# An attention and gated-layer kernel on one core: one decay transfer a pair, other places for conversions, x loads and second products

## The chip, the cores and the metric

The kernel runs on 1 core of one Trainium2 chip. The metric is the device time of one execution in microseconds (us). Times of the kernel before are the median of 3 runs, and one profiled execution stands beside them.

## The reference

```python
def _attn_ref(q, k, v, f):                     # q, k, v: (4, 8, 576, 64), f: (4, 8, 576)
    scores = (1 / np.sqrt(D)) * np.matmul(q, k.transpose(0, 1, 3, 2))
    cum = np.cumsum(np.log(np.clip(f, 0.0001, 1.0)), axis=-1)
    decay = cum[:, :, :, None] - cum[:, :, None, :]
    scores = np.where(causal, -1000000000.0, scores + decay)   # causal: np.triu(ones, k=1)
    attn = np.exp(scores - np.max(scores, axis=-1, keepdims=True))
    return np.matmul(attn / (np.sum(attn, axis=-1, keepdims=True) + 1e-09), v)

x = np.ascontiguousarray(attn_out.transpose(0, 2, 1, 3)).reshape(B * S, H * D)  # (2304, 512)
x = (1 / (1 + np.exp(-(x @ w_gate))) * (x @ w_val)) @ w_out                     # d_ff 1536
h = x @ w_in
return (h * np.clip(h + 3.0, 0.0, 6.0) / 6.0) @ w_out2                          # d_ff 2048
```

The weights come as float64 words, read as pairs of int32.

## The kernel before

Every product of the two layers is three matmuls (`mm3`, lines 453 to 455): high part times high part, high times low, low times high. So each weight tile and each activation exists as a high and a low half.

**Attention.** The 32 heads are 16 pairs. A pair has five query units: four of 128 rows (units 0 to 3) and a tail of 64 rows for each of the two heads (unit 4), which share one tile. The 80 units run in a software pipeline, one step t a unit: scores and exponentials of unit t, the division (`norm`, POOL, L382) of unit t-1, the transposes (`flip`) of unit t-2, the products with v (`values`) of unit t-3. Pairs 0 to 6 walk their units upwards, with the tail last; pairs 7 to 15 walk downwards, with the tail first. The decay needs the cumulated logarithms along the keys in every partition: `dc` [128, 2 x 512] for the four full units, filled by two broadcast DMAs a pair (L266), and `dt` [128, 576] for the tail, with one head in each half of the partitions, filled by two more (L274). `dt` has a single buffer, `dc` two. The first pass over the scores is the reduction at L350 on DVE, which adds `dc` or `dt` to the scores in PSUM and takes the minimum. In pairs 0 to 6 the causal mask is added by small bf16 matmuls (L336 for full units, L343 with `mask2` for the tail); in the others POOL writes it into `dc` and `dt` (`hide`, L316 and L311).

**Conversions.** A weight tile is converted by two jobs. A job is a DMA of the raw words (L100), three passes on DVE (L103, L104, L110), a scaling on ACT (L107), the high half on POOL or ACT (L61, L63) and the low half on POOL (L64). The raw tiles have three buffers. 16 jobs run beside attention (from step 17, 0.7 of a job a step), 20 more up to the first chunk of the gated layer, and 32 are for the second layer. In the gated layer `CB` gives the jobs a feature block: 2.0 in its first chunk and 0.5 in all others.

**Beside attention** the tensor engine also computes four of the twelve feature blocks of the gated layer for the token chunks 0 to 2 (the `Filler`), whose x comes back from DRAM after the stores of a batch (`fill.load`, L174).

**The two layers.** A chunk is 512 tokens, the last one 256. `layer` walks chunks and, in each, feature blocks of 128: the up products of block f (`ups`), then the down products of block f-1 (`last`). Between the two, ACT, DVE and POOL make the activation and split it into `gall`, a ring of three buffers. The gated layer goes through the chunks 3, 4, 0, 1, 2, the second layer through 3, 0, 1, 2, 4. `up2` and `downs` ask for their weight (`conv.need`), which issues what is left of the jobs up to it.

**What sets the order.** The text gives a program order; a scheduler that simulates the engines then places the instructions of each engine, and every engine executes its own in that order. All transfers named here are issued by SP, in one queue in order.

Of the kernel before, what the change touches and what calls it, by code (L numbers as in the profile page):

```python
# [7 lines left out]
F32 = mybir.dt.float32  # L8
F32R = mybir.dt.float32r
BF16 = mybir.dt.bfloat16  # L10
I32 = mybir.dt.int32
AF = mybir.ActivationFunctionType
ALU = mybir.AluOpType
# [3 lines left out]
BIG = 1.0e30  # L17
# [3 lines left out]
def attn_moe_kernel(  # L21
# [57 lines left out]
    )  # L79

    mask2 = const.tile([P, TAIL], BF16, name="mask2")
    nc.gpsimd.memset(mask2, 0.0)
    for g in range(2):
        nc.gpsimd.affine_select(
            out=mask2[64 * g : 64 * g + 64], in_=mask2[64 * g : 64 * g + 64],
            compare_op=ALU.is_ge, fill=BIG, base=0, pattern=[[-1, TAIL]], channel_multiplier=1,
        )

# [152 lines left out]
    class Pair:  # L241
# [13 lines left out]
        def load(self):  # L255

            new = lambda nm: nat.tile([P, NKT, 2, D], F32, tag="nat", name=nm)
            self.qn = load_nat(new("qn"), q, self.b, self.hp, ())
            self.kn = load_nat(new("kn"), k, self.b, self.hp, ((0, k), (TAIL, q)))
            self.vn = load_nat(vns[self.i % 3], v, self.b, self.hp, ((TAIL, v),))  # L260

        def load_decay(self):
            h0 = self.b * H + 2 * self.hp
            self.dc = a2.tile([P, 2, NQ * P], F32, tag="dc", name="dc")
            for j in range(2):
                nc.sync.dma_start(  # L266
                    self.dc[:, j, :], cum_d[h0 + j : h0 + j + 1, : NQ * P].to_broadcast([P, NQ * P])
                )

        def load_tail_decay(self):  # L270
            h0 = self.b * H + 2 * self.hp
            self.dt = a1.tile([P, S], F32, tag="dt", name="dt")
            for j in range(2):
                nc.sync.dma_start(  # L274
                    self.dt[64 * j : 64 * j + 64, :], cum_d[h0 + j : h0 + j + 1, :].to_broadcast([64, S])
                )
# [26 lines left out]
        def hide(self, s):  # L303


            if self.pemask:
                return
            if s == NQ:
                for j in range(2):
                    d = self.dt[64 * j : 64 * j + 64, NQ * P : S]  # L310
                    nc.gpsimd.affine_select(  # L311
                        out=d, in_=d, compare_op=ALU.is_ge, fill=BIG, base=0, pattern=[[-1, TAIL]], channel_multiplier=1
                    )
            else:
                d = self.dc[:, :, s * P : (s + 1) * P]
                nc.gpsimd.affine_select(  # L316
                    out=d, in_=d, compare_op=ALU.is_ge, fill=BIG, base=0, pattern=[[0, 2], [-1, P]], channel_multiplier=1
                )

        def scores(self, s):  # L320
# [18 lines left out]
            for c, st in enumerate(self.sts):  # L339
                masked = self.pemask and c == 1  # L340
                nc.tensor.matmul(st[:, :hs], self.qz, self.kp[:, c * hs : (c + 1) * hs], start=True, stop=not masked)
                if masked:
                    nc.tensor.matmul(st[:, hs - TAIL : hs], identb, mask2, start=False, stop=True)  # L343

# [249 lines left out]
    def layer(src, order, feats, ups, downs, finish, rate, first, more=None):  # L594
# [7 lines left out]
        load(order[0], KC)  # L602
        last = None
        for ci, c in enumerate(order):
# [5 lines left out]
            for f in fs:  # L610
                gt = gall[:, ring["g"] % 3, :, :T]
                ring["g"] += 1
                ups(f, loaded[c], gt, T)
                if nxt is not None and f == fs[-1]:
                    load(nxt, KC)
                if last:
                    last()

                def last(f=f, gt=gt, outs=outs, c=c, T=T, fs=fs):
                    downs(f, gt, outs, T, f == fs[0], f == fs[-1])  # L620
                    if f == fs[-1]:
                        finish(outs, c, *chunks[c])

                if more:
                    more(ci, f)
                conv.run(rate(ci), EF)
        last()

# [12 lines left out]
    def ff1(w, order, first):  # L641
# [34 lines left out]
        def more(ci, f):  # L676
            if ci == len(order) - NCA - 1 and f == 2 * NGA:
                next_weights(3 * NGA)
            if ci == len(order) - 1 and f % 2 == 1:
                next_weights(2 if f == 2 * NGA + 1 else 3)  # L680

        feats = lambda c: range(2 * NGA if c < NCA else 0, nf)
        layer(x_d, order, feats, ups, downs, finish, lambda ci: CB[min(ci, 1)], first, more)

# [44 lines left out]

    CA, C0, CF, CB, CC = 0.7, 17, 0.9, (2.0, 0.5), 1.5  # L730

# [23 lines left out]
    pairs[0].load_decay()  # L755
    pairs[0].load_tail_decay()
    warm_up(WU)
    pairs[0].prep()
    done = 0
    for t in range(len(units) + 3):  # L760
# [3 lines left out]
        if t < len(units):  # L764
# [3 lines left out]
            if i == 0 and nxt:  # L768
                nxt.load()
                nxt.load_decay()  # L770
            p.scores(s)
            p.expo(s)
            if s > 0:
                p.hide(s - 1)
            if nxt and i == (len(p.order) - 1 if p.up else 2):
                nxt.load_tail_decay()
            if nxt and i == len(p.order) - 1:
                nxt.hide(NQ)
        if 1 <= t <= len(units):
# [5 lines left out]
        if t >= 3:  # L785
# [3 lines left out]
            if s == p.order[-1]:  # L789
                p.store()  # L790

                fill.load(p.b, p.hp + 1)
                if p.hp == NP - 1 and p.b < NCA:
                    done = p.b + 1
        if t < len(units):
# [4 lines left out]
        if t >= C0:  # L800
            conv.run(CA, EA)
        fill.n = done
# [63 lines left out]
```

## Time and profile before

| | us |
|---|---|
| median of 3 runs (1100.93 to 1103.43) | 1102.96 |
| the profiled execution | 1099.57 |
| its span in the trace | 1097.8 |

The profiled execution is the one that the rows below come from. Its time is 1.8 us longer than the span, which runs from the first to the last event of the trace. The attention stage, with its filler, takes the first third of the span, the gated layer ends near 690 us, and the second layer follows to the end. A gap in square brackets at the end of a row is the idle time of that engine right before the instruction and what ended it. A matmul's duration includes its place in a pipeline: how many were done in a stretch says more than their mean length. In the rows of busy time, PEclk is the granted clock of the tensor engine as a share of full speed: 1.00 is 2.4 GHz and 0.50 is 1.2 GHz.

### The profile page before, as it was taken

The page shows a single profiled execution, that of the slowest core. Times are in us where ns is not written, and L with a number is a line of the kernel's source. Part 1 is how long each engine was busy: PE and PEld are TensorE (multiplying, and loading weights), DVE is VectorE, ACT ScalarE, POOL GpSimd, SP SyncE. Part 2 cuts the span into 40 slices and gives each one's busy share as a digit, 9 for nine tenths or more (in the row PEclk, how much of TensorE's full clock was granted, in tenths as well). Part 3 has the DMA queues.
Part 4 walks back from the last instruction along what each step waited for, and adds up shares of the span by engine and source line. Part 5 has one row for each costly group of instructions (what it writes and reads, how often), then busy time and mean ns, then how long its engine had stood idle before and what let it go on. Part 6 is the DMA issues. An engine that isn't in the chain of part 4 may idle for free.

```text
span 1097.8 us, 15036 instructions
## 1 busy us (share of the span) xinstructions
PE 1058.7 (96%) x5383; PEld 833.7 (76%) x5383; DVE 541.6 (49%) x1174; ACT 349.1 (32%) x790; POOL 251.4 (23%) x357
## 2 busy tenths in 40 slices
PE   8889989999999999999999999999999999999998
PEld 4556765766766778998888888876888888888897
DVE  5588676435434872625234251699433333333343
ACT  5666466457353430312112020244211111111121
POOL 3366565224323430212102020043000000000000
PEclk9899999999999999999999999999999999999999
DMA  7878666266234521405052250643300200110010
GB/s 185 256 197 257 207 208 181 85 168 173 73 130 137 152 79 38 175 18 194 1 169 100 77 173 16 225 139 121 106 10 1 84 31 1 58 39 1 20 39 19
DMA packets 111241, 119.09 MB, mean 108 GB/s; under 512 B 63232, under 2 KB 66304, under 8 KB 111168
## 3 DMA queue, kind: packets, MB, share of 16 engines
q1 hardware_dynamic: 111072, 118.00, 35.0%
q8 instruction: 42, 0.69, 0.3%
q14 instruction: 31, 0.25, 0.1%
q10 hardware_dynamic: 96, 0.15, 0.0%
HBM read 91.30 MB, written 26.81 MB: 108 GB/s over the span
## 4 chain that ended last, share of the span: by engine, by line
PE 76%; DVE 7%; DMA 6%; issue 4%; POOL 3%; ACT 2%; SPq 1%; ACTq 0%; POOLq 0%; DVEq 0%
PE po L454 9%; PE po L453 9%; PE po L455 9%; PE ph L453 5%; PE ph L454 5%; PE ph L455 5%; PE pv L453 4%; PE pv L454 4%; PE pv L455 4%; PE pv L439 4%; PE pg L453 4%; PE pg L454 4%; PE pg L455 4%; PE st L327 3%; PE tt L406 2%
## 5 line engine op out<-in xcount | busy, mean ns | idle before, releaser
L64 DVE TENSOR_TENSOR gall<-sg,gall 128x512 fp32r<-128x512 f32 (+1 forms) x140 | 96.0, 685 | 91.0 <-ACT gall L61 49.1
L61 ACT CAST gall<-sg 128x512 fp32r<-128x512 f32 (+1 forms) x80 | 46.2, 578 | 272.7 <-DVE sg L692 268.8
L691 DVE TENSOR_SCALAR sg<-ph 128x512 f32<-128x512 f32 (+1 forms) x80 | 50.9, 637 | 145.9 <-PE ph L455 145.7
L454 PE MATMUL ph<-x,wi 128*128 128x512 f32 (+1 forms) x320 | 117.9, 369 | 0.0
L455 PE MATMUL ph<-x,wi 128*128 128x512 f32 (+1 forms) x320 | 117.7, 368 | 0.0
L453 PE MATMUL ph<-x,wi 128*128 128x512 f32 (+1 forms) x320 | 117.0, 368 | 0.0
L453 PE MATMUL po<-w,gall 128*128 128x512 f32 x288 | 112.9, 393 | 2.0 <-ACT gall L61 1.9
L454 PE MATMUL po<-w,gall 128*128 128x512 f32 x288 | 113.0, 392 | 0.0
L382 POOL TENSOR_SCALAR e<-e,m 128x256 f32<-128x256 f32 (+4 forms) x144 | 84.4, 598 | 122.1 <-DVE m L380 60.3
L455 PE MATMUL po<-w,gall 128*128 128x512 f32 x288 | 102.8, 395 | 2.7 <-DVE gall L64 2.7
L358 ACT ACTIVATE e<-e,m 128x256 f32<-128x256 f32 (+4 forms) x144 | 83.9, 584 | 61.5 <-DVE m L350 55.5
L454 PE MATMUL po<-gall,wo 128*128 128x512 f32 (+1 forms) x240 | 89.9, 376 | 4.3 <-DVE gall L64 4.3
L650 DVE TENSOR_TENSOR sg<-sg,pv 128x512 f32<-128x512 f32 (+1 forms) x48 | 29.6, 617 | 128.2 <-PE pv L455 126.8
L453 PE MATMUL pg<-x,wg 128*128 128x512 f32 (+1 forms) x240 | 90.4, 379 | 2.1 <-ACT sg L648 2.1
L454 PE MATMUL pg<-x,wg 128*128 128x512 f32 (+1 forms) x240 | 89.8, 374 | 0.4 <-DMA x<-x_d 0.4
L455 PE MATMUL pg<-x,wg 128*128 128x512 f32 (+1 forms) x240 | 89.8, 374 | 0.0
L453 PE MATMUL pv<-x,wv 128*128 128x512 f32 (+1 forms) x240 | 89.3, 372 | 0.0
L454 PE MATMUL pv<-x,wv 128*128 128x512 f32 (+1 forms) x240 | 89.0, 371 | 0.0
L453 PE MATMUL po<-gall,wo 128*128 128x512 f32 (+1 forms) x240 | 87.9, 374 | 1.0 <-POOL gall L63 1.0
L455 PE MATMUL pv<-x,wv 128*128 128x512 f32 (+1 forms) x240 | 88.8, 370 | 0.0
L455 PE MATMUL po<-gall,wo 128*128 128x512 f32 (+1 forms) x240 | 88.5, 371 | 0.0
L63 POOL TENSOR_SCALAR gall<-sg 128x512 fp32r<-128x512 f32 (+1 forms) x60 | 39.1, 653 | 214.6 <-DVE sg L650 207.5
(110 smaller groups left out, 1921.3 us busy)
## 6 DMA issues: line engine op xcount, KB each, us to landing
x<-x_d SPq DMA_DIRECT2D x88, 256.0 KB, 3.7
raw<-in_moe_w_out_dram SPq DMA_DIRECT2D x28, 512.0 KB, 3.6
x_d<-x SPq DMA_DIRECT2D x32, 288.0 KB, 2.9
dc<-cum_d SPq DMA_DIRECT2D x32, 256.0 KB, 4.3
x_d<-xs SPq DMA_DIRECT2D x32, 256.0 KB, 3.3
raw<-in_moe_w_in_dram SPq DMA_DIRECT2D x16, 512.0 KB, 4.4
raw<-in_moe_w_gate_dram SPq DMA_DIRECT2D x12, 512.0 KB, 4.0
raw<-in_moe_w_val_dram SPq DMA_DIRECT2D x12, 512.0 KB, 4.5
```

Source lines behind the costliest of these rows:

```text
L61: nc.scalar.copy(hi, src)
L63: eng_hi.tensor_scalar(hi, src, 1.0, 1.0, ALU.mult, ALU.mult)
L64: eng_lo.tensor_tensor(lo, src, hi.bitcast(F32), ALU.subtract)
L327: mm = nc.tensor.matmul(st[:, :n], self.qp[r, qs], self.kp[r, :n], start=True, stop=not self.pemask)
L358: nc.scalar.activation(e, e, AF.Exp, bias=m[:, a : a + 1], scale=-1.0, accum_out=m[:, 2 + b : 3 + b])
L382: nc.gpsimd.tensor_scalar(e, e, m[:, 6 + j : 7 + j], 1.0, ALU.mult, ALU.mult)
L439: row(nc.tensor.matmul(o[64 * j : 64 * j + 64, q0:], self.vn[:, kt, j], e, start=(kt == 0), stop=(kt == nk - 1)), kt == 0 and j == 0)
L453: nc.tensor.matmul(o, wh, xh, start=first, stop=False)
L454: nc.tensor.matmul(o, wh, xl, start=False, stop=False)
L455: nc.tensor.matmul(o, wl, xh, start=False, stop=last)
L650: nc.vector.tensor_tensor(sg, sg, pv, ALU.mult)
L691: nc.vector.tensor_scalar(sg, ph, 3.0, 0.0, ALU.add, ALU.max)
```

## The change

One DMA a pair now brings both heads' 576 columns into `dc` (L260 of the changed kernel). `dt` is no longer transferred: `tail_decay` makes it from `dc` with two POOL selects of 64 x 576 a pair, in all pairs, which write the tail's mask at once, so `mask2`, its matmuls and the tail's `hide` go. The v loads stand behind the decay. The filler's x is fetched two steps later. Conversions in attention start at step 14, and the last four of the 16 come at 0.09 a step. In both layers the down products come two blocks behind the up products, with four buffers of `gall`. The gated layer's chunks convert 2.0 (first), 0.5 and, in the last, 2.5 jobs a feature block.

```diff
...
-    mask2 = const.tile([P, TAIL], BF16, name="mask2")
-    nc.gpsimd.memset(mask2, 0.0)
-    for g in range(2):
-        nc.gpsimd.affine_select(
-            out=mask2[64 * g : 64 * g + 64], in_=mask2[64 * g : 64 * g + 64],
-            compare_op=ALU.is_ge, fill=BIG, base=0, pattern=[[-1, TAIL]], channel_multiplier=1,
-        )
...
+        def load_v(self):
...
-            self.dc = a2.tile([P, 2, NQ * P], F32, tag="dc", name="dc")
-            for j in range(2):
-                nc.sync.dma_start(
-                    self.dc[:, j, :], cum_d[h0 + j : h0 + j + 1, : NQ * P].to_broadcast([P, NQ * P])
-                )
+            self.dc = a2.tile([P, 2, S], F32, tag="dc", name="dc")
+            both = cum_d[h0 : h0 + 2].rearrange("h s -> (h s)").rearrange("(o x) -> o x", o=1)
+            nc.sync.dma_start(self.dc.rearrange("p h s -> p (h s)"), both.to_broadcast([P, 2 * S]))
+        def tail_decay(self):
...
-        def load_tail_decay(self):
-            h0 = self.b * H + 2 * self.hp
...
-                nc.sync.dma_start(
-                    self.dt[64 * j : 64 * j + 64, :], cum_d[h0 + j : h0 + j + 1, :].to_broadcast([64, S])
+                r = slice(64 * j, 64 * j + 64)
+                nc.gpsimd.affine_select(
+                    out=self.dt[r], in_=self.dc[r, j], compare_op=ALU.is_ge, fill=BIG, base=NQ * P,
+                    pattern=[[-1, S]], channel_multiplier=1,
...
-            if self.pemask:
-                return
-            if s == NQ:
-                for j in range(2):
-                    d = self.dt[64 * j : 64 * j + 64, NQ * P : S]
-                    nc.gpsimd.affine_select(
-                        out=d, in_=d, compare_op=ALU.is_ge, fill=BIG, base=0, pattern=[[-1, TAIL]], channel_multiplier=1
-                    )
-            else:
+            if not self.pemask:
...
-                masked = self.pemask and c == 1
-                nc.tensor.matmul(st[:, :hs], self.qz, self.kp[:, c * hs : (c + 1) * hs], start=True, stop=not masked)
-                if masked:
-                    nc.tensor.matmul(st[:, hs - TAIL : hs], identb, mask2, start=False, stop=True)
+                nc.tensor.matmul(st[:, :hs], self.qz, self.kp[:, c * hs : (c + 1) * hs], start=True, stop=True)
...
-        last = None
+        late = []
...
-                gt = gall[:, ring["g"] % 3, :, :T]
+                gt = gall[:, ring["g"] % 4, :, :T]
...
-                if last:
-                    last()
+                if len(late) > 1:
+                    late.pop(0)()
...
+                late.append(last)
...
-        last()
+        for last in late:
+            last()
...
-            if ci == len(order) - NCA - 1 and f == 2 * NGA:
+            if ci == len(order) - NCA - 1 and f == 2 * NGA + 1:
...
-        layer(x_d, order, feats, ups, downs, finish, lambda ci: CB[min(ci, 1)], first, more)
+        layer(x_d, order, feats, ups, downs, finish, lambda ci: CB[0] if ci == 0 else CB[1] if ci < len(order) - 1 else CB[2], first, more)
...
-    CA, C0, CF, CB, CC = 0.7, 17, 0.9, (2.0, 0.5), 1.5
+    CA, C0, CF, CB, CC = 0.7, 14, 0.9, (2.0, 0.5, 2.5), 1.5
+    CS = 0.09
...
-    pairs[0].load_tail_decay()
+    pairs[0].load_v()
+    pairs[0].tail_decay()
...
+                nxt.load_v()
...
-                nxt.load_tail_decay()
-            if nxt and i == len(p.order) - 1:
-                nxt.hide(NQ)
+                nxt.tail_decay()
...
-                fill.load(p.b, p.hp + 1)
...
+        if t >= 5:
+            p, s = units[t - 5]
+            if s == p.order[-1] and t < len(units) + 3:
+                fill.load(p.b, p.hp + 1)
...
-            conv.run(CA, EA)
+            conv.run(CA if len(conv.jobs) > 2 * NSA - 6 * NGA else CS, EA)
```

Three places show how the order moves. In the rows, names and lines are each kernel's own, and "x2" is two alike in a row.

**SP, among the loads of the third to fifth pairs.** `qn`, `kn` and `vn` are loads for attention, `x_d` a store of attention's result, `x` the filler's load. Before:

```order
L266 DMA dc<-cum_d 128x512 x2
L231 DMA qn<-in_q_dram 128x4x64
L274 DMA dt<-cum_d 64x576 x2
L174 DMA x<-x_d_93 128x512
L231 DMA qn<-in_q_dram 128x4x64
L174 DMA x<-x_d_94 128x512
L266 DMA dc<-cum_d 128x512 x2
```

Changed:

```order
L260 DMA dc<-cum_d 128x1152
L223 DMA qn<-in_q_dram 128x4x64 x2
L92 DMA raw<-in_moe_w_gate_dram 128x2x512 x2
L92 DMA raw<-in_moe_w_val_dram 128x2x512
L260 DMA dc<-cum_d 128x1152
L223 DMA vn_133<-in_v_dram 128x4x64 x2
L432 DMA x_d_85<-x 128x576
```

The two `dt` transfers are gone from between the loads, `dc` is one DMA, and the filler's x no longer stands here.

**POOL, in the pairs that walk downwards.** `e<-e,m` is the division of a unit, by its width (576 is the tail); `dc<-dc` and `dt` are the masks. Before:

```order
L382 TENSOR_SCALAR e<-e,m 128x256 x2
L382 TENSOR_SCALAR e<-e,m 128x128 x2
L382 TENSOR_SCALAR e<-e,m 128x576
L316 AFFINE_SELECT dc<-dc 128x2x128
L382 TENSOR_SCALAR e<-e,m 128x512 x2
L316 AFFINE_SELECT dc<-dc 128x2x128
L311 AFFINE_SELECT dt<-dt 64x64 x2
L316 AFFINE_SELECT dc<-dc 128x2x128
```

Changed:

```order
L366 TENSOR_SCALAR e<-e,m 128x256 x2
L366 TENSOR_SCALAR e<-e,m 128x128 x2
L366 TENSOR_SCALAR e<-e,m 128x576
L268 AFFINE_SELECT dt<-dc 64x576 x2
L303 AFFINE_SELECT dc<-dc 128x2x128 x2
L366 TENSOR_SCALAR e<-e,m 128x512 x2
L303 AFFINE_SELECT dc<-dc 128x2x128
```

Two selects of 64 x 576 now stand behind the tail's division and in front of the next unit's, where two of 64 x 64 stood one unit later.

**DVE, the gated layer's last chunk.** `sg<-sg,pv` and `gall<-sg,gall` are a feature block's activation and its low half, `raw<-raw` the passes of conversions. Before:

```order
L650 TENSOR_TENSOR sg<-sg,pv 128x512
L64 TENSOR_TENSOR gall<-sg,gall 128x512
L650 TENSOR_TENSOR sg<-sg,pv 128x512
L64 TENSOR_TENSOR gall<-sg,gall 128x512
L650 TENSOR_TENSOR sg<-sg,pv 128x512
L64 TENSOR_TENSOR gall<-sg,gall 128x512
```

Changed:

```order
L636 TENSOR_TENSOR sg<-sg,pv 128x512
L102 SCALAR_TENSOR_TENSOR raw<-raw 128x512
L64 TENSOR_TENSOR gall<-sg,gall 128x512
L95 TENSOR_SCALAR raw<-raw 128x512
L96 SCALAR_TENSOR_TENSOR raw<-raw 128x512
L95 TENSOR_SCALAR raw<-raw 128x512
L102 SCALAR_TENSOR_TENSOR raw<-raw 128x512
L96 SCALAR_TENSOR_TENSOR raw<-raw 128x512
L95 TENSOR_SCALAR raw<-raw 128x512
L96 SCALAR_TENSOR_TENSOR raw<-raw 128x512
L102 SCALAR_TENSOR_TENSOR raw<-raw 128x512
L636 TENSOR_TENSOR sg<-sg,pv 128x512
```

Before, five feature blocks at the end of this chunk have no conversion between them; now seven to eight passes stand between the activations of two blocks. The jobs left for the second layer's first chunk go from 17 to 4, and 16 stand in this chunk.

## Rows read from the trace of the kernel before

**Rows 1.** Page, parts 1 and 4: busy time by engine; shares of the last chain.

```profile
PE 1058.7 (96%) x5383; PEld 833.7 (76%) x5383; DVE 541.6 (49%) x1174; ACT 349.1 (32%) x790; POOL 251.4 (23%) x357
...
PE 76%; DVE 7%; DMA 6%; issue 4%; POOL 3%; ACT 2%; SPq 1%; ACTq 0%; POOLq 0%; DVEq 0%
```

**Rows 2.** Stretches: from:to, length, busy of PE PEld DVE ACT POOL, PEclk, DMA, GB/s.

```profile
47.50:54.30 6.80, 6.62 (x32) 4.70 (x32) 3.40 (x16) 3.95 (x11) 3.67 (x7) 0.50 0.83 238
50.00:100.00 50.00, 43.75 (x283) 28.33 (x279) 39.65 (x121) 34.76 (x97) 29.30 (x39) 0.96 0.82 234
...
372.00:404.00 32.00, 27.74 (x118) 21.42 (x116) 28.59 (x35) 13.81 (x23) 15.45 (x13) 1.00 0.42 130
455.00:472.00 17.00, 16.01 (x131) 15.60 (x130) 13.22 (x19) 6.54 (x12) 7.67 (x8) 1.00 0.17 59
640.00:695.00 55.00, 55.00 (x244) 45.60 (x243) 17.26 (x25) 8.71 (x14) 8.69 (x10) 1.00 0.27 87
720.00:770.00 50.00, 45.40 (x185) 34.96 (x184) 45.64 (x64) 22.57 (x35) 20.52 (x14) 0.97 0.41 127
850.00:900.00 50.00, 50.00 (x222) 41.46 (x221) 18.63 (x27) 7.77 (x13) 0.00 (x0) 1.00 0.19 63
```

**Rows 3.** Timeline from 41 to 48 us: start, length, engine, line, idle before.

```profile
41.57 1.11 SPq L274 DMA_DIRECT2D dt<-cum_d  x2
...
46.13 0.46 DVE L350 CUSTOM_DVE_ANT_0 e<-st,dt 128x288 f32<-128x288 f32 x1 [4.17 <-DMA dt<-cum_d]
...
47.67 1.09 PE L400 MATMUL tt<-ident,e 128*128 128x128 f32 x4 [2.61 <-DVE qp L288]
```

**Rows 4.** Timeline from 131 to 146 us, where the walking order turns.

```profile
131.48 8.09 SPq L274 DMA_DIRECT2D dt<-cum_d  x4
...
137.23 0.46 DVE L350 CUSTOM_DVE_ANT_0 e<-st,dt 128x288 f32<-128x288 f32 x1 [1.98 <-DMA dt<-cum_d]
...
141.82 0.66 PE L413 MATMUL tt<-ident,e 128*128 128x128 f32 x4 [0.80 <-POOL e L382]
...
144.99 0.33 PE L415 MATMUL t<-ident,e 128*128 128x128 f32 x1 [1.10 <-ACT etB L419]
```

**Rows 5.** Waits: who waited for whom: us in total, times, longest.

```profile
DVE e L350 <- DMA dt<-cum_d: 6.1, 2, 4.2
...
PE po L454 <- DVE gall L64: 4.3, 6, 1.7
...
PE po L455 <- DVE gall L64: 2.7, 2, 1.6
```

**Rows 6.** Timeline around 702 and 768 us: first and last of 17 jobs.

```profile
702.70 0.33 SPq L100 DMA_DIRECT2D raw<-in_moe_w_out_dram  x1
...
768.51 1.31 POOL L64 TENSOR_TENSOR w<-raw,w 128x512 fp32r<-128x512 f32 x1 [2.79 <-ACT w L61]
```

**Rows 7.** DVE's groups: shape, count; busy us, mean ns; idle before.

```profile
L104 DVE SCALAR_TENSOR_TENSOR raw<-raw 128x512 int32<-128x512 int32 x68 | 64.0, 942 | 1.4
L110 DVE SCALAR_TENSOR_TENSOR raw<-raw 128x512 int32<-128x512 int32 x68 | 57.6, 848 | 16.3 <-ACT raw L107 16.2
L103 DVE TENSOR_SCALAR raw<-raw 128x512 int32<-128x512 int32 x68 | 43.4, 639 | 29.4 <-DMA raw<-in_moe_w_in_dram 14.0 <-DMA raw<-in_moe_w_gate_dram 10.0 <-DMA raw<-in_moe_w_out_dram 3.9
```

**Rows 8.** POOL's groups, in the same form.

```profile
L316 POOL TENSOR_SCALAR_AFFINE_SELECT dc<-dc 128x256 f32<-128x256 f32 x36 | 15.6, 434 | 46.2 <-DVE m L350 28.5 <-DMA dc<-cum_d 12.6 <-issue 2.1
L382 POOL TENSOR_SCALAR e<-e,m 128x576 f32<-128x576 f32 x16 | 13.7, 854 | 16.3 <-DVE m L380 7.9 <-ACT etA L419 5.1 <-ACT e L358 1.9
...
L311 POOL TENSOR_SCALAR_AFFINE_SELECT dt<-dt 64x64 f32<-64x64 f32 x18 | 5.1, 284 | 3.1 <-DMA dt<-cum_d 2.8
```

**Rows 9.** The mask matmuls of the tail, in the same form.

```profile
L343 PE MATMUL st<-mask,identb 128*128 128x64 bf16 x7 | 1.4, 193 | 0.0
```

**Rows 10.** L104 on DVE: duration in ns, least, median and greatest.

```profile
L104 DVE SCALAR_TENSOR_TENSOR raw<-raw x68: 678/694/1819, 64.1 to 765.1; 128x512 int32<-128x512 int32 x68
```

**Rows 11.** DMA issues: count, KB each, median us from issue to landing.

```profile
dc<-cum_d SPq DMA_DIRECT2D x32, 256.0 KB, 4.3
```

## The prediction, made before the changed kernel was run

> **What bounds the kernel now.** First the page. TensorE is busy 96% of the span, and the chain that ended last runs over it for 76%; DVE, DMA, issue and POOL share most of the rest [rows 1]. Busy time of pipelined matmuls hides small gaps, so I read stretches next, and count matmuls in them. From 850 to 900 us, where only 128 x 512 matmuls run and nothing is late, 222 start in 50 us: 0.2252 us each [rows 2]. From 640 to 695 us there are 244 in 55 us, the same pitch, so the last chunk of the gated layer has no gap, although 0.5 of a job a block is converted there [rows 2]. Against this pitch the other stretches show what is lost. From 720 to 770 us there are 185 matmuls, worth 41.7 us: 8.3 of 50 us are lost, while DVE is busy for 45.6 of them [rows 2]. From 372 to 404 us there are 118, worth 26.6 of 32: 5.4 lost; from 455 to 472 us 131, among them 256-wide ones, with PE busy for 16.0 of 17: 1.0 lost [rows 2]. Attention has shorter and mixed instructions, so there I read the timeline: DVE waits 4.2 us for the transfer of `dt` that SP issued at 41.57, and PE then has a gap of 2.6 us ahead of 47.67 [rows 3]. Right behind it, from 47.5 to 54.3, the granted clock is 0.50, the level of 1.2 GHz [rows 2]. The second such wait, 2.0 us at 137 us, stands where pair 6 (tail last) meets pair 7 (tail first) and both want the one `dt` [rows 4]. The two make up 6.1 us in the list of waits [rows 5]. Everything not named here I take to stay.
>
> **The change, part by part**, against the profiled execution's own 1099.57 us.
>
> *The tail's transfer goes.* At the first place the gap of 2.6 us goes with the wait [rows 3]. The slow stretch behind it: 32 matmuls in 6.6 us of PE at half the clock; from 50 to 100 us, at 0.96, 283 take 43.75, or 0.155 each, which makes 4.9 for 32 [rows 2]. So 1.7 us return if the clock does not fall; bounded by nothing (another gap brings the fall back) and 3.4 (half of 6.8). Term: -4.3, between 0 and -6.0. At the second place the select of pair 7 must still wait until the tail of pair 6 has read `dt`, but then takes two POOL instructions and no transfer. What PE waits for around it is 0.8 and 1.1 us [rows 4]. Term: -1.9, between 0 and -1.9. The other pairs show no such wait [rows 5], so there a faster `dt` frees nothing. One DMA of `dc` in place of two, with 1152 columns in place of 1024: its 4.3 us [rows 11] lie a whole pair ahead of use. I take nothing. If its landing comes late, it costs what `dt` cost (the first rival but one).
>
> *POOL makes the tail's decay.* Per pair two selects of 64 x 576. No row has the shape: from 64 columns (284 ns) to 256 (434 ns) the slope is 0.78 ns a column, which puts 576 at 0.68 us; the division of 128 x 576 takes 0.85 [rows 8]. 32 of them are 22 to 27 us, less the 18 that go (5.1 us): POOL gets 17 to 22 us more, where it is busy for 29.3 of 50 us at the densest [rows 2]. What stands behind them in POOL's order is the next unit's division, for which the transposes wait. If each pair's two, 1.4 to 1.7 us, lay on the path in all 16 pairs, that were 22 to 27 us. In the rows PE meets POOL's division only now and then, at 0.8 us in the row shown [rows 4], because the pipeline gives a unit's division a whole step until the transposes. Term: +2 (one or two pairs in which they stand in the way), between 0 and +27; the row nearest is the 0.8, hence the low value.
>
> *The tail's mask.* Seven matmuls of 0.19 us go, 1.4 us at most [rows 9]. They lie in the dense score stretch, but the reduction behind them was what PE waited for; term 0, between 0 and -1.4.
>
> *Down products two blocks later.* The lost 5.4 and 1.0 us of the stretches from 372 and 455 [rows 2] are of one kind: a block's down products come right behind the next block's up products and wait for the last half of `gall` from DVE (4.3 and 2.7 us over the whole trace [rows 5]), while DVE is busy for 28.6 of 32 us with conversions in between [rows 2]. With another whole block of up products between, 24 matmuls or 5.4 us, the same chain has time. The list names 7.0 us of such waits; what the two stretches lose is 6.4. I take -5.0, between 0 and -6.4: something of the first stretch is waiting for weights, which this edit doesn't hasten. The price is one more buffer of `gall`, and one more block of down products at the very end, of the same number of matmuls.
>
> *Conversions to the last gated chunk.* By the order, the second layer's first chunk has 17 jobs left before and 4 now. Before, they ran from 702.70 to 769.8, 67.1 us, or 3.95 us a job [rows 6]. The second layer eats four jobs in two blocks, 48 matmuls or 10.8 us at the pitch: 2.7 a job. So it is held back by the converting, and the 8.3 us are the outcome. With 4 left, nothing holds it. The jobs' new place: a block of the last chunk has 36 matmuls, 8.1 us, in which 2.5 jobs come. A job on DVE is 0.94 + 0.85 + 0.64 = 2.43 us [rows 7], so 6.1 a block, and DVE's other work there is 17.3 of 55 us, 2.5 a block [rows 2]; that 17.3 has a few of the old jobs in it, so 8.1 of 8.1 is too much by their share. It is tight, but two blocks of slack lie behind each activation now, and what does not fit only slides on into the second layer. Term: -6.5 of the 8.3, between 0 and -8.3. It counts on the activation not falling behind the conversions in DVE's order.
>
> *The rest.* The filler's x two steps later: it leaves SP's queue free around the store, and its user comes a batch later; 0. Earlier and thinner conversions in attention: the same 16 jobs, 0. The scheduler puts much else elsewhere, which no row prices; I allow 3 us either way.
>
> Sum: -4.3 - 1.9 + 2 - 5.0 - 6.5 = -15.7, which makes 1083.9 for a profiled execution. The median of before lies 3.4 above its profiled one (1102.96 against 1099.57), so about **1087** as a median.
>
> On the same resources, the trace shows that a pass of the conversions, L104, takes 0.69 us as a rule and up to 1.82 [rows 10]: at times it stands still for as long as another instruction takes. The Trainium skill ("SBUF — State Buffer", section "Who interferes with whom") says that a DVE instruction with two SBUF inputs and a GpSimd one that reads SBUF shut each other out, the second to issue waiting for the whole of the first. The trace agrees: L104 has two such inputs, and the 1.1 us above the usual 0.69 are the length of a POOL instruction. By the row alone the passes keep their mean, and the sum stands; by the rule each of the 32 selects can hold a DVE instruction for its own 0.68 to 0.85 us, 22 to 27 us of DVE in all, which would carry the time to that of the slower rival below if PE waited for DVE each time.
>
> **The rivals.**
>
> *The stall only moves* (conversions too dense). For: at the 3.95 us a job of the old place [rows 6], 2.5 jobs are 9.9 us a block of 8.1, which over the eight blocks of the chunk is 14 us too much; raw tiles have three buffers as before. Against: there POOL, ACT and DVE also served a layer with shorter blocks, and what slides has slack. What does not fit slides into the second layer at the old pace, the 6.5 shrink to nothing, and the sum is -9.2: 1090.4 profiled, about 1094.
>
> *The wait changes its name.* `dc` now carries the tail too, and a select waits for it on POOL, in front of the next divisions. For: the transfers are dense in the first 100 us (DMA share 0.82 [rows 2]), where `dt` was late. Against: it is issued a pair ahead. Then -4.3 and -1.9 are lost: 1090.1 profiled, about 1093.5.
>
> *POOL's selects come onto the path* (slower). The place is attention, the price 1.4 to 1.7 us a pair. It decides if the selects delay the division in all pairs and POOL's queue never catches up: +22 to +27 in place of +2, so +4 to +9 in sum, 1104 to 1109 profiled, about 1110 as a median. It outweighs the 17.7 us of gains from some 11 pairs on. For: selects stand right in front of divisions in the order, and DMA waits move to POOL. Against: POOL is idle for 20 of 50 us there [rows 2].
>
> *The edits do not do it*: the scheduler places the later down products and the conversions so that PE still meets the same waits. Then only the first term remains, 1095.3 profiled, about 1099.
>
> **How the numbers follow.** The forecast 0.53, its own range from 1080 to 1092. The stall moves 0.14, about 1094. The wait changes its name 0.12, about 1093. POOL on the path 0.13, about 1110. The edits do not do it 0.08, about 1099, a part of which lies within 0.2% (2.2 us, about what a measurement here can tell from no change). Faster by more than that: 0.53 + 0.14 + 0.12 and a part of the last, 0.81; same 0.06; slower 0.13. The range goes from 1076 (all upper bounds of the gains, 24.0 us, give 1079; the scheduler's 3 below it) to 1104, which leaves out most of the slower rival.
>
> **What would show it.** In the changed trace: no gap ahead of PE near 41 to 54 us and no granted clock of 0.50 there; no DVE wait at the first reduction of pair 7's tail for a transfer; 118 matmuls in some 27 us in the first gated chunk; in the last gated chunk 0.2252 us a matmul still, with DVE nearly full; and 222 matmuls in 50 us from the second layer's start on. Wrong it would be if POOL's selects head the list of what transposes wait for, if waits for `gall` show in the last gated chunk, or if the second layer begins with DVE busy for 45 of 50 us again.

## The result, and the profile after

| | before | changed |
|---|---|---|
| median of 4 runs, us | 1102.09 (1100.93 to 1103.43) | 1086.14 (1084.18 to 1086.25) |
| profiled execution's span, us | 1097.8 | 1082.4 |

The changed kernel is faster: the ratio is 0.9845, 95% interval 0.9827 to 0.9864. The forecast of 1087 us lies within a microsecond of it. Its parts don't: two gains were larger than predicted, and one, of 6.5 us, isn't there at all.

The page's parts 1 and 4 of the changed kernel (busy time by engine; shares of the last chain) answer to [rows 1]:

```profile
PE 1055.0 (97%) x5376; PEld 831.7 (77%) x5376; DVE 543.4 (50%) x1174; ACT 349.5 (32%) x790; POOL 273.7 (25%) x368
...
PE 82%; DVE 5%; DMA 5%; issue 3%; POOL 3%; ACT 2%; SPq 0%; ACTq 0%; POOLq 0%; DVEq 0%
```

POOL is busy for 22.3 us more: 17.5 are the new selects less those that went, and 5.0 are divisions that take longer (89.4 us in place of 84.4). PE's share of the chain rose. The stretches of the changed kernel (columns as in [rows 2]) say where:

```profile
41.00:54.00 13.00, 11.57 (x87) 7.04 (x83) 10.73 (x39) 9.24 (x28) 6.46 (x10) 1.00 0.89 231
50.00:75.00 25.00, 19.60 (x129) 11.16 (x127) 21.08 (x68) 18.48 (x55) 21.22 (x25) 0.93 0.81 235
131.00:146.00 15.00, 15.00 (x89) 10.00 (x89) 6.91 (x24) 8.63 (x22) 9.10 (x14) 1.00 0.27 83
360.00:392.00 32.00, 32.00 (x143) 26.48 (x142) 27.58 (x34) 13.07 (x22) 13.07 (x12) 1.00 0.48 153
440.00:460.00 20.00, 20.00 (x169) 20.00 (x169) 14.38 (x21) 7.04 (x13) 7.68 (x8) 1.00 0.35 121
622.00:650.00 28.00, 28.00 (x125) 23.17 (x125) 18.56 (x26) 8.73 (x14) 8.01 (x6) 1.00 0.66 213
650.00:665.00 15.00, 15.00 (x68) 12.43 (x67) 12.81 (x16) 5.70 (x9) 7.19 (x6) 1.00 0.46 149
665.00:690.00 25.00, 20.39 (x77) 15.62 (x76) 18.84 (x27) 10.67 (x17) 10.98 (x9) 0.86 0.66 220
712.00:762.00 50.00, 50.00 (x221) 41.08 (x220) 25.82 (x37) 9.42 (x15) 2.88 (x2) 1.00 0.01 4
```

At the pitch of 0.2252 us a matmul, the first gated chunk (360 to 392) and the turn of 440 to 460 lose nothing, and the second layer's start (712 to 762) loses 0.2 us, where before it lost 8.3 [rows 2]. But the end of the last gated chunk, gapless before, loses 7.7: 77 matmuls are worth 17.3 of its 25 us. The clock no longer falls at 41 to 54 us, and PE is busy throughout from 131 to 146. Attention's last product with v starts at 326.2 us, 7.6 earlier than the 333.8 of before. So the account of the two traces is: attention -7.6, the first gated chunk and the turn -6.4, the second layer's start -8.1, the last gated chunk +7.7. That makes -14.4 of the 15.4 us by which the spans differ.

The wait of the tail's reduction, [rows 5], in the changed kernel:

```profile
POOL dt L268 <- DMA dc<-cum_d: 21.8, 5, 9.9
...
ACT e L342 <- POOL dt L268: 1.5, 1, 1.5
...
DVE e L334 <- POOL dt L268: 0.6, 1, 0.6
```

The waiting for a transfer moved to POOL's selects, as a rival had it, but they are early enough: ACT and DVE wait for them once each, for 1.5 and 0.6 us. 9.9 of the 21.8 us are the first pair's, at the kernel's start.

How the 7.7 us are lost shows in the timeline of the changed kernel: DVE's activations (`sg`) and PE's waits between 640 and 690 us.

```profile
649.84 0.67 DVE L636 TENSOR_TENSOR sg<-sg,pv 128x512 f32<-128x512 f32 x1
659.60 0.68 DVE L636 TENSOR_TENSOR sg<-sg,pv 128x512 f32<-128x512 f32 x1
670.69 0.68 DVE L636 TENSOR_TENSOR sg<-sg,pv 128x512 f32<-128x512 f32 x1
673.34 0.49 PE L437 MATMUL po<-gall,wo 128*128 128x512 f32 x1 [1.95 <-POOL gall L63]
676.09 0.79 PE L438 MATMUL po<-gall,wo 128*128 128x512 f32 x1 [2.25 <-DVE gall L64]
679.94 0.68 DVE L636 TENSOR_TENSOR sg<-sg,pv 128x512 f32<-128x512 f32 x1
```

The products that these four activations read started their last matmul at 643.8, 652.0, 660.1 and 668.3 us. So the activation comes 6.0, 7.6, 10.6 and 11.6 us behind: it falls back from block to block until the slack of two blocks is used up, and PE waits for both halves of `gall`, at a clock that then falls as well.

### The profile page after: what moved, and what is told of

It is laid out like the page before. It is cut to its first block, busy times and chain, and to the rows that moved or that the text cites. A ratio compares the mean times of both kernels' runs of the same rounds, so it can differ in the third digit from the quotient of the medians.

```text
span 1082.4 us, 14927 instructions
## 1 busy us (share of the span) xinstructions
PE 1055.0 (97%) x5376; PEld 831.7 (77%) x5376; DVE 543.4 (50%) x1174; ACT 349.5 (32%) x790; POOL 273.7 (25%) x368
## 4 chain that ended last, share of the span: by engine, by line
PE 82%; DVE 5%; DMA 5%; issue 3%; POOL 3%; ACT 2%; SPq 0%; ACTq 0%; POOLq 0%; DVEq 0%
PE po L438 10%; PE po L439 9%; PE po L437 9%; PE ph L439 6%; PE ph L438 6%; PE ph L437 6%; PE pv L423 5%; PE st L314 4%; PE pv L438 3%; PE pv L437 3%; PE pv L439 3%; PE pg L439 3%; PE pg L438 3%; PE pg L437 3%; PE tt L390 2%
## 5 line engine op out<-in xcount | busy, mean ns | idle before, releaser
L438 PE MATMUL po<-w,gall 128*128 128x512 f32 x288 | 112.2, 390 | 0.0
L437 PE MATMUL po<-w,gall 128*128 128x512 f32 x288 | 112.1, 390 | 0.0
L439 PE MATMUL po<-w,gall 128*128 128x512 f32 x288 | 111.4, 389 | 0.0
L366 POOL TENSOR_SCALAR e<-e,m 128x256 f32<-128x256 f32 (+4 forms) x144 | 89.4, 634 | 75.1 <-DVE m L364 38.8
L438 PE MATMUL po<-gall,wo 128*128 128x512 f32 (+1 forms) x240 | 90.7, 379 | 2.7 <-DVE gall L64 2.7
L437 PE MATMUL po<-gall,wo 128*128 128x512 f32 (+1 forms) x240 | 89.7, 378 | 1.9 <-POOL gall L63 1.9
L439 PE MATMUL po<-gall,wo 128*128 128x512 f32 (+1 forms) x240 | 90.0, 377 | 0.0
```

The lines of the kernel that those rows point to most:

```text
L366: nc.gpsimd.tensor_scalar(e, e, m[:, 6 + j : 7 + j], 1.0, ALU.mult, ALU.mult)
L437: nc.tensor.matmul(o, wh, xh, start=first, stop=False)
L438: nc.tensor.matmul(o, wh, xl, start=False, stop=False)
L439: nc.tensor.matmul(o, wl, xh, start=False, stop=last)
```

## Experiments

Each time is a median, with the ratio to the runs of before in the same group. Losses of a stretch are its length less its matmuls times 0.2252 us.

**The decay part alone**, put into the kernel before (one DMA of `dc` a pair, two selects that make `dt`, no `mask2`; all else as before). A part of the edit:

```diff
...
-            self.dc = a2.tile([P, 2, NQ * P], F32, tag="dc", name="dc")
...
+            self.dc = a2.tile([P, 2, S], F32, tag="dc", name="dc")
...
-                nxt.load_tail_decay()
-            if nxt and i == len(p.order) - 1:
-                nxt.hide(NQ)
+                nxt.tail_decay()
...
```

> The kernel before with the decay part alone: one transfer a pair, the tail's decay by POOL selects, no mask2; v loads, x loads, conversions and down products as before. Theory A (the decay made the attention stage shorter): nearly all of the 7.7 us by which attention ended earlier in the changed kernel is here, about 1095 us, no DVE wait for a dt transfer, the last product with v near 326 us. Rival B (the moved x loads, v loads or conversions did it): 1099 or more, attention's end at 330 us or later.

1091.94 us, ratio 0.9894 (0.9877 to 0.991): 11.7 us. Attention's last product with v starts at 324.7. So theory A holds, and more than it asked for. Between the two profiled executions the difference is smaller, 7.2 us of span (1097.8 and 1090.6): attention ends 9.1 us earlier, and the layers take 2 us longer. The kernel before and this one, from 50 to 75 us:

```profile
50.00:75.00 25.00, 20.99 (x141) 12.76 (x138) 17.95 (x65) 17.99 (x53) 11.49 (x17) 0.91 0.82 225
```

```profile
50.00:75.00 25.00, 22.90 (x158) 14.27 (x158) 22.35 (x67) 18.82 (x56) 19.59 (x26) 1.00 0.76 225
```

There are 17 more matmuls, and the clock stays up throughout, while the prediction had priced its fall at the one place around 47 us only.

**The later down products alone**, put into the kernel before (with the fourth buffer of `gall` and the later `next_weights` that they need). A part of the edit:

```diff
...
-                if last:
-                    last()
+                if len(late) > 1:
+                    late.pop(0)()
...
```

> The kernel before with the down products two blocks later and four gall buffers alone. Theory: the stretches of the first gated chunk lose nothing any more (6.7 us come back) and 0.4 us at the end, about 1095 us; the second layer's start still loses 8 us. Rival (the first chunk waits for weights or conversions): half of it or less, 1099 or more.

1090.84 us, ratio 0.9884 (0.987 to 0.9899): 12.8 us, more than the theory. The first gated chunk and the second layer's start:

```profile
374.00:402.00 28.00, 28.00 (x125) 23.21 (x124) 23.04 (x29) 12.19 (x21) 11.89 (x10) 1.00 0.46 149
...
725.00:775.00 50.00, 48.02 (x201) 38.33 (x201) 38.54 (x56) 18.52 (x29) 14.13 (x10) 0.97 0.41 130
```

The first loses nothing. The second loses 4.7 us where before lost 8.3: the block of slack covers part of the conversion stall as well, which neither the theory nor the prediction had. These are 10.0 us; from the gated layer's first product to the end of the span, the two profiled executions differ by 11.3 (763.8 and 752.5).

**The denser conversions alone**, put into the kernel before:

```diff
-        layer(x_d, order, feats, ups, downs, finish, lambda ci: CB[min(ci, 1)], first, more)
+        layer(x_d, order, feats, ups, downs, finish, lambda ci: CB[0] if ci == 0 else CB[1] if ci < len(order) - 1 else CB[2], first, more)
...
-    CA, C0, CF, CB, CC = 0.7, 17, 0.9, (2.0, 0.5), 1.5
+    CA, C0, CF, CB, CC = 0.7, 17, 0.9, (2.0, 0.5, 2.5), 1.5
```

> The kernel before with 2.5 jobs a block in the last gated chunk alone; down products one block later as before. Theory (the stall only moves: 2.5 jobs a block hold the activation up in DVE's order): the 8.4 us at the second layer's start come back, and at least as much is lost in the last gated chunk, since only one block of slack is there: 1102 to 1112 us. Rival (the denser conversions are hidden, as predicted): about 1095 us.

1106.33 us, ratio 1.0025 (1.0007 to 1.0042): slightly slower. Its last gated chunk, the second layer's start, and PE's waits in the former:

```profile
675.00:715.00 40.00, 35.12 (x142) 26.98 (x141) 32.14 (x44) 16.21 (x26) 17.27 (x14) 0.96 0.54 177
720.00:770.00 50.00, 50.00 (x222) 41.17 (x221) 27.12 (x41) 10.76 (x17) 5.54 (x4) 1.00 0.18 59
```

```profile
PE po L454 <- DVE gall L64: 3.6, 3, 1.8
PE po L453 <- POOL gall L63: 1.2, 2, 0.7
```

8.0 of 40 us are lost in the one (142 matmuls are worth 32.0) and none in the other. The stall moved, with its size: 8.3 us at the second layer's start before, 8.0 in the last gated chunk now.

**The changed kernel with 0.5 jobs in the last gated chunk.**

```diff
-    CA, C0, CF, CB, CC = 0.7, 14, 0.9, (2.0, 0.5, 2.5), 1.5
+    CA, C0, CF, CB, CC = 0.7, 14, 0.9, (2.0, 0.5, 0.5), 1.5
```

> The changed kernel with 0.5 jobs a block in the last gated chunk, as before. Theory (the stall only moves): 8 us come back in the last gated chunk and about 8.4 are lost at the second layer's start, so the time stays within 2 us of the changed kernel's 1086. Rival (this edit is worth the predicted 6.5 us): about 1092.5 us.

1084.28 us (1081.78 to 1086.4), against 1086.14 and, in the next group, 1086.6 for the changed kernel: the edit is worth nothing, or costs a little. The last gated chunk and the second layer's start:

```profile
625.00:675.00 50.00, 50.00 (x222) 41.41 (x221) 18.87 (x28) 9.22 (x15) 8.99 (x9) 1.00 0.37 123
...
712.00:762.00 50.00, 47.43 (x199) 37.87 (x199) 43.02 (x62) 21.37 (x33) 17.23 (x12) 0.97 0.33 106
```

Nothing is lost in the first, 5.2 us in the second. In the changed kernel it is 7.7 and 0.2. So by these stretches the denser conversions cost 2.7 us, and by the medians 2.

**The small edits.** The changed kernel again as a reference, the two large parts together without the rest, and the changed kernel with one small edit undone each:

```diff
f2:
-    CA, C0, CF, CB, CC = 0.7, 14, 0.9, (2.0, 0.5, 2.5), 1.5
+    CA, C0, CF, CB, CC = 0.7, 17, 0.9, (2.0, 0.5, 2.5), 1.5
...
-            conv.run(CA if len(conv.jobs) > 2 * NSA - 6 * NGA else CS, EA)
+            conv.run(CA, EA)

f3:
...
+                fill.load(p.b, p.hp + 1)
...
-        if t >= 5:
-            p, s = units[t - 5]
-            if s == p.order[-1] and t < len(units) + 3:
-
-                fill.load(p.b, p.hp + 1)
...
```

In f3 the load stands right behind the store, two steps earlier.

> The changed kernel again, as a reference for the others of this group: 1084 to 1088 us.

> The kernel before with the decay part and the later down products together, without the other edits. If the two add (they took 11.7 and 12.8 us alone): about 1079 us, some 6 us below the changed kernel, and the edits left out cost what is missing. If they share their gain (rival): 1084 to 1086, and the edits left out cost nothing.

> The changed kernel with the conversions in attention as before (from step 17, 0.7 a step throughout). Theory (early conversions meet the tail's selects on POOL): PE's wait of 3.0 us at 66 us for a division that stands behind two conversion passes and two selects is gone, and the time is 2 to 4 us below the changed kernel's. Rival (the start is free): within 1 us of it.

> The changed kernel with the filler's x fetched right behind the store, as before. Predicted at nothing: within 2 us of the changed kernel. Rival (the later fetch keeps SP's queue free for the decay): 2 us or more above it.

| run | median, us | lowest to highest |
|---|---|---|
| the changed kernel again | 1086.60 | 1085.73 to 1088.27 |
| decay and downs alone (f1) | 1081.29 | 1079.18 to 1083.89 |
| old start of conversions (f2) | 1084.10 | 1082.53 to 1087.07 |
| x behind the store (f3) | 1089.75 | 1086.27 to 1093.28 |

The two parts almost add: 20.5 of 24.5 us (ratio 0.9805, 0.9762 to 0.9848). The other edits together cost 5.3 us. From the gated layer's first product to the end of the span, f1 takes 752.1 us and the changed kernel, in its two profiles, 756.0 and 755.3. So 3 to 4 us lie behind attention, most of them the cost of the denser conversions. The early start may take the rest: its medians differ by 2.5 us, as the theory had it, but the runs overlap, so this isn't shown. Its mechanism is seen. In the changed kernel, POOL and PE around 66 us:

```profile
63.76 1.09 POOL L63 TENSOR_SCALAR wv<-raw 128x512 fp32r<-128x512 f32 x1
64.93 1.30 POOL L64 TENSOR_TENSOR wv<-raw,wv 128x512 fp32r<-128x512 f32 x1
66.19 1.85 POOL L268 TENSOR_SCALAR_AFFINE_SELECT dt<-dc 64x576 f32<-64x576 f32 x2
68.13 1.92 POOL L366 TENSOR_SCALAR e<-e,m 128x576 f32<-128x576 f32 x3
68.98 0.66 PE L397 MATMUL tt<-ident,e 128*128 128x128 f32 x4 [3.01 <-POOL e L366]
```

The tail's division stands behind two conversion passes and two selects, and PE waits 3.0 us. The same wait of 3.0 us, with 129 matmuls from 50 to 75 us, stands in the second profile of the changed kernel. With the old start, the corresponding wait is 0.8 us, and 161 matmuls start:

```profile
50.00:75.00 25.00, 22.91 (x161) 14.08 (x158) 21.96 (x67) 19.17 (x56) 19.52 (x26) 1.00 0.78 226
```

The later x fetch seems to help by 3 us, against my nothing; the runs are too wide apart to be sure. The new place of the v loads was not tried by itself.

**Between 0.5 and 2.5 jobs a block**, with the old start of conversions in attention:

```diff
-    CA, C0, CF, CB, CC = 0.7, 14, 0.9, (2.0, 0.5, 2.5), 1.5
+    CA, C0, CF, CB, CC = 0.7, 17, 0.9, (2.0, 0.5, 1.0), 1.5
...
-            conv.run(CA if len(conv.jobs) > 2 * NSA - 6 * NGA else CS, EA)
+            conv.run(CA, EA)
```

The second run has 1.5 in place of 1.0.

> The changed kernel with the conversions in attention as before and 1.0 job a block in the last gated chunk in place of 2.5. Theory (at 2.5 the last gated chunk loses 8 us, at 0.5 the second layer's start loses 5; between them both fit): at most 3 us lost in both places together, 1079 to 1081 us. Rival (what is taken from one place is lost in the other at any rate): 1082 to 1085 us.

> As the run before, with 1.5 jobs a block. Theory: 1077 to 1080 us, less than 2 us lost in both places together. Rival: 1082 to 1085 us.

1077.01 us (ratio 0.9779, 0.9754 to 0.9804) with 1.0, and 1078.54 (1077.34 to 1083.19) with 1.5. With 1.0, the last gated chunk and the second layer's start:

```profile
640.00:680.00 40.00, 40.00 (x178) 33.16 (x177) 22.72 (x30) 10.40 (x17) 11.05 (x11) 1.00 0.37 129
720.00:770.00 50.00, 49.90 (x219) 40.73 (x218) 29.57 (x45) 14.34 (x23) 6.89 (x5) 1.00 0.24 78
```

0.7 us is lost in both together. The stall need not be conserved: each place has some room, and the load fits when it is divided between both. At 1.5 the last gated chunk loses 4.7 us again, at least in the profiled execution, which is the slowest of the four (1083.19 us):

```profile
640.00:690.00 50.00, 47.43 (x201) 38.57 (x200) 35.89 (x46) 16.69 (x27) 18.11 (x15) 0.97 0.51 168
```

The number in `CB` does not set how densely the jobs come. In the changed kernel, at 1.5 and at 1.0 they run one right behind the other: the first passes on DVE start 3.62, 3.57 and 3.36 us apart (14 jobs from 641.58 to 688.58 us, 10 from 638.56 to 670.69, 7 from 633.89 to 654.05). What differs is how many come in a row. Seven make the activation at most 6.2 us late, counted from the start of the last matmul that it reads, and PE never waits; with ten it is 11.0 us late, and PE waits 1.3 us for each half of `gall`.

**Activation first.** The changed kernel, 2.5 jobs a block, with the order on DVE bound:

```diff
...
-            split_sbuf(gt[:, 0], gt[:, 1], sg, nc.gpsimd, nc.vector)
+            pace["dve"] = split_sbuf(gt[:, 0], gt[:, 1], sg, nc.gpsimd, nc.vector)
...
```

`convert` places its first pass behind the instruction in `pace["dve"]`, here the low half of the block issued ahead of it. The passes may still stand in front of the next block's activation.

> The changed kernel, 2.5 jobs a block as there, where the first pass of a conversion may not be placed on DVE before the low half of the gated block issued ahead of it. If the order on DVE holds the activation up (passes that stand ahead of an activation wait for DMA and ACT while it could run): half or more of the 8 us of the last gated chunk comes back, 1082 us or less. Rival (too many passes for the block's 8.1 us, in whatever order): 1085 to 1088 us.

1081.31 us (1079.74 to 1086.58). The median is that of the theory, though one of the four runs is as slow as the changed kernel; the place is another. The gated layer's first blocks and the last gated chunk of this run:

```profile
330.00:345.00 15.00, 15.00 (x68) 12.43 (x67) 7.37 (x13) 4.54 (x8) 1.76 (x3) 1.00 0.23 70
650.00:690.00 40.00, 35.86 (x150) 28.40 (x149) 31.21 (x43) 16.42 (x27) 17.57 (x14) 0.96 0.53 182
```

The last gated chunk still loses 6.2 us. That does not decide between theory and rival, since the edit did not bring the activation forward there: nine passes stand between the activations at 635.47 and 646.48 us, and as many up to the next at 656.22. An order with the activation in front was not tried.

What came back is a wait that I had not looked at, for the first blocks' sigmoid at the gated layer's start. It is gone here, and still stands in the run with one job a block. That run's DVE, ACT and PE, and its stretch:

```profile
336.21 0.43 DVE L95 TENSOR_SCALAR raw<-raw 128x512 int32<-128x512 int32 x1 [9.01 <-DMA raw<-in_moe_w_gate_dram]
337.46 0.68 ACT L99 ACTIVATE raw<-raw 128x512 f32<-128x512 f32 x1 [9.03 <-DVE raw L96]
339.44 1.09 ACT L634 ACTIVATE sg<-pg 128x512 f32<-128x512 f32 x2
340.10 0.50 PE L437 MATMUL pg<-x,wg 128*128 128x512 f32 x1 [2.67 <-ACT sg L634]
```

```profile
330.00:345.00 15.00, 12.33 (x47) 9.70 (x46) 7.78 (x12) 5.58 (x8) 4.75 (x5) 0.89 0.49 168
```

ACT's queue holds a conversion's scaling in front of the sigmoid. The scaling waits 9.0 us for DVE's passes, and these for the transfer of the raw words. With the lower clock, 4.4 of the 15 us are lost. The stall is as old as the kernel before: of the 20 us that begin 2 us behind the gated layer's first product, before and changed kernel lose 3.8 each (72 matmuls), and the prediction, whose stretches begin later, does not have it.

**One job a block and activation first**: both diffs above, the old start of conversions among them.

> The kernel with one job a block and the old start of conversions, and with the order of the run before last's third (no first pass of a conversion ahead of the low half of the block issued before it). Theory (that order only takes the 2.3 us wait for the sigmoid away at the gated layer's first block, and the rest adds): 1073 to 1076 us. Rival (the order pushes conversions later, and the second layer's start waits for them again): 1077 us or more.

1070.47 us (1068.93 to 1075.7, 6 runs), ratio 0.971 (0.9684 to 0.9736), the best version here: 33 us below before and some 16 below the changed kernel. Its gated layer's start, last gated chunk and second layer's start:

```profile
330.00:345.00 15.00, 15.00 (x68) 12.43 (x67) 9.10 (x14) 5.19 (x9) 3.83 (x4) 1.00 0.14 46
640.00:680.00 40.00, 40.00 (x178) 33.11 (x177) 19.78 (x33) 10.92 (x18) 8.97 (x9) 1.00 0.39 131
720.00:770.00 50.00, 49.80 (x218) 40.58 (x218) 27.08 (x41) 13.26 (x22) 5.39 (x4) 1.00 0.24 83
```

It is below what the theory gave (1073 to 1076). The theory took 2.3 us for the sigmoid's wait; the whole place, with its lower clock, cost 4.4 in the run with one job a block and costs nothing here. The rest, about 2 us of the medians, is open and may be the spread of attention between executions (last section). In the last gated chunk the order helps here too: the seven jobs, except the first three, start 6 to 8 us apart, and the activation is at most 3.0 us late.

## Why the prediction was right in sum and wrong in parts

**Conversions, -6.5: the step failed.** It priced a job at DVE's 2.43 us and compared 6.1 us a block, and the rest, with the block's 8.1. Its own sum was too high: 6.1 and the 2.5 of DVE's other work make 8.6, not 8.1, and 7.6 without the three old jobs in that row, so DVE's work alone would just have fitted. The price of a job was right: in the last gated chunk of the changed kernel (612 to 690 us) DVE's passes are

```profile
L96 DVE SCALAR_TENSOR_TENSOR raw<-raw 128x512 int32<-128x512 int32 x15 | 14.6, 975 | 0.4
L102 DVE SCALAR_TENSOR_TENSOR raw<-raw 128x512 int32<-128x512 int32 x15 | 11.8, 787 | 5.4 <-ACT raw L99 5.4
L95 DVE TENSOR_SCALAR raw<-raw 128x512 int32<-128x512 int32 x16 | 11.0, 689 | 5.6 <-DMA raw<-in_moe_w_out_dram 2.3 <-DMA raw<-in_moe_w_in_dram 1.9 <-POOL wi L64 1.2
```

The three means add to 2.45 us a job. But a job's pace is that of its whole chain, and DVE's order makes everything behind a waiting pass wait too. The last two rows carry that waiting, for ACT, for the raw words, for a buffer: 11.0 us. The first passes of 14 jobs start at

```profile
641.58 1.48 DVE L95 TENSOR_SCALAR raw<-raw 128x512 int32<-128x512 int32 x1
...
688.58 0.43 DVE L95 TENSOR_SCALAR raw<-raw 128x512 int32<-128x512 int32 x1 [0.18 <-DMA raw<-in_moe_w_out_dram]
```

which is 47.0 us for 13 intervals, 3.62 us a job. The same measure gives 3.58 for the 17 jobs of before at the second layer's start (first passes from 706.78 to 764.12), which [rows 6], from the first transfer to the last pass, put at 3.95. 2.5 jobs are 9.0 us in a block of 8.1, and the activation, behind them in DVE's order, falls back until PE waits. By that price 1.5 jobs (5.4 us) would fit in a block; in the profiled execution they did not, and there they come in a row and not evenly. The edit was worth nothing: with it the time is, if anything, 2 us longer, not 6.5 shorter. The rival "the stall only moves" had the pace and the lost 6.5, and I gave it 0.14; but it put the loss into the second layer, where 0.2 us are lost, and its time of 1094 was not met. One of the prediction's own signs of being wrong, waits for `gall` in the last gated chunk, did show. SP's waits from 640 to 690 us name what holds the next raw tile, POOL's low half that frees its buffer:

```profile
SPq L92 <- POOL wi L64: 19.2, 7, 4.3
SPq L92 <- POOL w L64: 14.4, 6, 4.7
```

Whether a fourth raw buffer would speed the chain up was not tried.

**The tail's transfer, -4.3 and -1.9: right in kind, too small.** The waits and the low clock of [rows 2 to 4] are gone. Alone, the whole decay part took 11.7 us off the median (9.9 to 13.6), and 7.2 between the profiled executions, not 4.2 (the two terms less the 2 us for POOL). I had read one stall and the turn, and taken the rest to stay; the stretch from 50 to 75 us gained 17 matmuls. The scheduler placed much anew there, so what of this is the transfer, and what the new order, stays open.

**POOL's selects, +2: right.** 32 of them at 0.705 us is 22.6 us, at the lower end of the 0.68 to 0.85 taken:

```profile
L268 POOL TENSOR_SCALAR_AFFINE_SELECT dt<-dc 64x576 f32<-64x576 f32 x32 | 22.6, 705 | 39.9 <-DMA dc<-cum_d 21.8 <-DVE m L334 9.9 <-DVE m L363 3.7
```

They held PE up once, for 3.0 us at 69 us, and that with two conversion passes in front, which the earlier start had put there. The slower rival had the mechanism; it needs it in 11 pairs.

**Down products, -5.0: right place, too small.** The gated layer gave back all of its 6.4 us, and the same slack took 3.6 us off the second layer's start, which I had booked under conversions alone. So the two edits were not independent: with the slack there, only about 5 us of the 8.3 were left for the conversions to win. The medians' 12.8 us are some 1.5 more than the traces show behind attention.

**The rest at nothing.** The earlier start of conversions may cost 2.5 us, and the later x fetch may bring 3; neither is settled beyond its runs' spread.

Together: from the -15.7, 7.5 us more by the decay, 7.8 more by the down products, 6.5 not had by the conversions and 4.0 that the first two share make -20.5, which is what the two parts measured together. The other edits took 5.3 of it back, and -15.2 is left, against a measured -16.0. The forecast was met by luck: the misses cancel.

## What to carry to other kernels

Price added work by the pace at which its whole chain ran in the nearest stretch (first pass to last, over the intervals), not by the busy time of its busiest engine, and ask how many jobs come in a row, not how many the code asks for on average: seven at this pace were covered by two blocks of slack, ten were not. A queue executed in order hands each wait of the chain to all that stands behind it, as the activation on DVE and the sigmoid on ACT show. When a stall is fed by too little time for a fixed amount of work, moving all of the work moves the stall, and dividing it between both places can remove it. Ask of each edit which other stall its slack also covers, since such gains do not add.

## What the runs showed of the hardware

The same attention program does not take the same time in each execution: in two profiled executions of the changed kernel its last product with v starts at 326.2 and 329.0 us, though the later stages are equal to within 1 us. With a single pair of profiles, a difference of 3 us in that stage says nothing; the medians of several runs do. A gap of 2 to 3 us brought the clock down in some places and not in others: it was 0.86 from 665 to 690 us and 0.93 from 50 to 75 us in the changed kernel, with its gaps at 671 to 676 and 66 to 69, but 1.00 from 70 to 80 us in the profile of before, where PE waited 2.7 us at 72.9. At one and the same place, the gated layer's start, a wait of 2.0 us for the sigmoid stands in 20 us at 0.91 (down products alone, from 337.9 us) and one of 2.8 in 20 us at 1.00 (old start of conversions, from 327.45). So the price of a gap above its own length can't be told from one profile.
